# A gated mix of window attention and a gated MLP at decode: larger output-weight pieces, a one-row gate load, another order of two waits

## The chip, the cores and the metric

The kernel runs on one NeuronCore of a Trainium2 chip. The metric is the device time of one execution in microseconds (us). The kernel before takes 196.78 us, the median of four runs (196.64, 196.65, 196.91 and 196.96 us).

## The reference

One token per batch entry (B = 4, width 512) goes through two branches, and a scalar gate mixes them:

```python
g = sigmoid((x * gate_w).sum(-1))            # x: [4, 1, 512], gate_w: [512]
q = x @ wq                                   # 32 heads of 128; 8 key/value heads
k, v = the last 4096 rows of k_cache, v_cache
a = softmax(q k^T / sqrt(128)) v @ wo        # wq: [512, 4096], wo: [4096, 512]
b = (relu(x @ W_gate) * (x @ W_up)) @ W_down # 512 -> 1792 -> 512
out = g * a + (1 - g) * b                    # [4, 1, 512]
```

All tensors are bf16. The kernel reads 81 MB, nearly all of it the window of the two caches (8 blocks of 4 MB each for K and for V), wq and wo (4 MB each), and the three MLP matrices (1.8 MB each).

## The kernel before

The four engines and the SyncE queue (SP) each have a program written out in one fixed order (`_order` for the engines, `_dma_order` for SP), with semaphores between them. Every load is issued by SP on one queue. The order of the loads is: wq, x, gate_w, K0, K1, V0, then K and V blocks by turns up to K7 and V6, then W_gate and W_up, V7, W_down, and wo in pieces. A load of a block waits until its slot is free (four slots of 32 KB a partition in `slots`); the pieces of wo and W_down go to slots that came free long before.

Each block `s` holds four heads for one batch entry. VectorE (DVE) transposes K in four quarters (`EKT`, L492), TensorE (PE) makes the scores (`SC`), DVE adds a mask and takes the maximum (`ESC`, L528), ScalarE (ACT) takes the exponential (`EXP`, L620), DVE transposes the result (`EPT`, L543), and PE multiplies by V (`PV`, L394 by way of the helper at L321). One block's PV is issued while the next block's scores are made.

The start: `XT` (L334) transposes x with four small PE transposes into PSUM, `EXT` (L495) copies the result to `xT`, with four columns for each of the four quarters `q` of the width. ACT spreads gate_w over 128 columns (`GWB`, L600), and `Z` (L340) multiplies that by xT, which gives the logit of the gate on all partitions. Then `Q` (L345) makes the queries. PE runs these strictly in that order: CONST, XT, Z, Q. gate_w comes in as `gwT`, four elements (8 bytes) on each of 128 partitions.

The end: after block 7's scores PE runs `PV` of block 6, the fold of the row sums (`RS`), the two MLP products (`GU`), `PV` of block 7, `FFN` (the product with W_down, accumulated into a PSUM bank), `OQ` (brings the heads' outputs into the layout that wo needs), and `WO`: 64 matmuls with 256 columns each, numbered x = 0 to 63, that accumulate on FFN's result. `WO_PIECES` (L28) cuts these 64 into seven groups, and each group has a load of its own and waits for it alone (L427). A step of x is 512 bytes of every partition's row of wo, so the pieces are 8, 8, 8, 4, 2, 1.5 and 0.5 KB a partition. The last piece is loaded in three parts of 123, 3 and 2 partitions (`LOW3`). Last, ACT and DVE copy one half of the sum each to `osum` (`FIN`, L623 and L577), and SP issues the store (L285), which waits for both.

`E.wait` (L61) makes one wait for each semaphore, in the order in which the keys are given. In the program as it runs, the second of the store's two waits stands alone as an instruction ahead, and the first is carried by the store's own issue: the profile has a separate wait for DVE, and then the issue, which waits for ACT's semaphore.

Of the kernel before, what the change touches and what calls it, by code (L numbers as in the profile page):

```python
# [6 lines left out]
BF16 = mybir.dt.bfloat16  # L7
ACTF = mybir.ActivationFunctionType
# [16 lines left out]
OUTT = 2  # L25
OW = 512 // OUTT
OR = 128 // OUTT
WO_PIECES = ((0, 16), (16, 32), (32, 48), (48, 56), (56, 60), (60, 63), (63, 64))  # L28
LOW3 = (0, 123, 126, 128)

class _Plan:
# [18 lines left out]
def bc(ap, axis, n):  # L50
    shape = list(ap.shape)
    shape[axis] = n
    return ap.broadcast_to(shape)
# [49 lines left out]
def _alloc(nc, ctx):  # L103
    R = {}

    def sb(name, shape, dt):
        R[name] = ctx.enter_context(nc.sbuf_tensor(name, shape, dt))

    sb("slots", [128, NSLOT, 16384], BF16)
    sb("kt", [128, 4, 4096], BF16)  # L110
    sb("sc", [128, 2048], BF16)
    sb("pe", [128, 2048], BF16)
    sb("pT", [128, 2, 2048], BF16)
    sb("qblk", [128, NSET, 2, 144, 2], BF16)
    sb("xsb", [4, 512], BF16)
    sb("xT", [128, 16], BF16)
    sb("gwT", [128, 4], BF16)
    sb("osb", [128, NSET, 512], BF16)
    sb("oq", [128, 32, 4], BF16)
    sb("identb", [128, 128], BF16)  # L120
    sb("identf", [128, 128], FP32)
    sb("ones", [128, 128], FP32)
    sb("ee", [16, 128], BF16)
    sb("e4", [16, 128], BF16)
    sb("rfold", [128, 128], FP32)
    sb("grpb", [128, 128], BF16)
    sb("own8", [128, 8], FP32)
    sb("scl", [128, 8], FP32)
    sb("maskl", [128, 128], BF16)
    sb("maskr", [128, 512], BF16)  # L130
    sb("maskf", [128, 512], BF16)
    sb("gwB", [128, 4, 128], BF16)
    sb("fold", [128, 4, 4, 64], BF16)
    sb("mx4", [128, 4], FP32)
    sb("rd32", [128, 8, 4], BF16)
    sb("negmax", [128, 2], FP32)
    sb("rowsum", [128, NSET], FP32)
    sb("recip", [128, 4, 4], FP32)
    sb("ge", [128, 2, 4], FP32)
    sb("gp", [128, 2, 4], FP32)  # L140
    sb("gg", [128, 2, 4], FP32)
    sb("hg", [128, 14, 4], BF16)
    sb("osum", [4, 512], BF16)
    R["psum"] = ctx.enter_context(nc.psum_tensor("bank", [128, 8, 512], FP32))
    return R


def _order():
# [7 lines left out]
    o += [("SC", s, 3), ("SW", s), ("PV", s - 1), ("PT", s), ("RS", 1), ("GU",), ("PV", s), ("FFN",), ("OQ",)]  # L156
    return o + [("WO", p) for p in range(len(WO_PIECES))]


def _dma_order():  # L160
    o = [("wq",), ("x",), ("gw",), ("k", 0), ("k", 1), ("v", 0)]
    for s in range(2, NSET):
        o += [("k", s), ("v", s - 1)]
    return o + [("wg",), ("wu",), ("v", NSET - 1), ("wd",)] + [("wo", p) for p in range(len(WO_PIECES))]

# [22 lines left out]
def _program(nc, plan, R, aps):  # L188
    (A_x, A_k_cache, A_v_cache, A_wq, A_wo, B_W_gate, B_W_up, B_W_down, gate_w, out) = aps
    banks = [R["psum"][:, i, :] for i in range(8)]  # L190
    bankb = [b.bitcast(BF16) for b in banks]
    TR, SCB, ACC, OB = (0, 1), (2, 3, 4), 5, (6, 7)
    slots, kt, sc, pe, pT, qblk = R["slots"], R["kt"], R["sc"], R["pe"], R["pT"], R["qblk"]
    xsb, xT, gwT, osb, oq = R["xsb"], R["xT"], R["gwT"], R["osb"], R["oq"]
    identb, identf, ones = R["identb"], R["identf"], R["ones"]
    mx4, rd32, negmax, rowsum, recip = R["mx4"], R["rd32"], R["negmax"], R["rowsum"], R["recip"]
    ge, gp, gg, osum = R["ge"], R["gp"], R["gg"], R["osum"]
# [5 lines left out]
    def slot(*it):  # L203
        return slots[:, at[it], :]

    Wq = slot("wq").rearrange("p (t f) -> p t f", t=4)
# [22 lines left out]
    def tr(key):  # L229
        return TR[trf[key] % NTR]  # L230

    def tr_free(key):
        n = trf[key] - NTR
        return [("E",) + trk[n]] if n >= 0 else []

    def scb(key):
        return SCB[scf[key] % NSC]
# [5 lines left out]
    def wo_rows(p):  # L243

        return [slice(a, b) for a, b in zip(LOW3, LOW3[1:])] if p == len(WO_PIECES) - 1 else [slice(0, 128)]

# [6 lines left out]
    def sync(e):  # L253
        E = _Eng(plan, e, "sp")

        def load(ev, ctr, dst, src, waits=()):
            E.op(lambda: e.dma_start(dst, src), ev=ev, waits=waits, ctr=ctr)  # L257

        for it in _dma_order():
            k = it[0]  # L260
            w = slot_wait.get(it, [])
            if k == "x":
                load(("X",), "d_x", xsb[0:4, :], A_x.rearrange("b o d -> (b o) d"))
            elif k == "gw":
                load(("GW",), "d_gw", gwT[:, :], gate_w.rearrange("(p t) -> p t", t=4))
            elif k == "wq":
                load(("WQ",), "d_wq", slot("wq"), A_wq.rearrange("(p t) f -> p (t f)", t=4), waits=w)
            elif k == "wg":
                load(("WG",), "d_wg", Wg, B_W_gate.rearrange("(p t) f -> p (t f)", t=4), waits=w)
            elif k == "wu":  # L270
                load(("WU",), "d_wu", Wu, B_W_up.rearrange("(p t) f -> p (t f)", t=4), waits=w)
            elif k == "wd":
                load(("WD",), "d_wd", Wd, B_W_down.rearrange("(p i) c -> p (i c)", i=14),
                     waits=w)
            elif k == "wo":
                lo, hi = WO_PIECES[it[1]]
                wo = A_wo.rearrange("(p i) c -> p (i c)", i=32)
                for n, r in enumerate(wo_rows(it[1])):
                    load(("WO", it[1], n), f"d_wo{it[1]}", Wo[r, OW * lo:OW * hi], wo[r, OW * lo:OW * hi], waits=w)
            else:  # L280
                b, qq = set_of(it[1])
                src = (A_k_cache if k == "k" else A_v_cache)[b, 4 * qq:4 * qq + 4, SK - WIN:SK, :]
                load((k.upper(), it[1]), f"d_{k}{it[1] % 3}", slot(*it), src.rearrange("h (r c) d -> r h (c d)", r=32),
                     waits=w)
        load(("OUT",), "d_out", out.rearrange("b o d -> (b o) d"), osum[:, :], waits=[("OSUM", 0), ("OSUM", 1)])  # L285
        E.wait([("OUT",)])

    def gpsimd(e):
# [28 lines left out]
    def tensor(t):  # L317
        E = _Eng(plan, t, "pe")

        def mm(out_, lhsT, rhs, start, stop, ev=None, waits=(), pos=None):  # L320
            E.op(lambda: t.matmul(out_, lhsT, rhs, start=start, stop=stop, tile_position=pos, skip_group_check=True),  # L321
                 ev=ev, waits=waits)

        def tp(out_, in_, idn, ev=None, waits=()):
            E.op(lambda: t.transpose(out_, in_, idn), ev=ev, waits=waits)  # L325
# [8 lines left out]
        def XT():  # L334
            bk = bankb[tr(("XT",))]
            for q in range(4):
                tp(bk[:, 4 * q:4 * q + 4], xsb[0:4, q:q + 509:4], identb[0:4, 0:4], ev=("XT",) if q == 3 else None,
                   waits=tr_free(("XT",)) + [("X",), ("IDB",)])

        def Z():  # L340
            for q in range(4):
                mm(banks[ACC][:, 0:4], R["gwB"][:, q, :], xT[:, 4 * q:4 * q + 4], q == 0, q == 3, ev=("Z",) if q == 3 else None,
                   waits=[("E", "XT"), ("GWB",), ("INIT",)])

        def Q():  # L345
            for n in range(2):
                key = ("Q", n)
                for q in range(4):
                    for j in range(4):
                        c = (4 * n + j) * 512  # L350
                        mm(banks[scb(key)][32 * j:32 * j + 4, :], xT[:, 4 * q:4 * q + 4], Wq[:, q, c:c + 512],
                           q == 0, q == 3, ev=key if (q, j) == (3, 3) else None, pos=(0, 32 * j),
                           waits=sc_free(key) + [("WQ",), ("E", "XT"), ("INIT",)] if (q, j) == (0, 0) else ())

# [52 lines left out]
        def GU():  # L407
            for n, (W, key) in enumerate(((Wg, "WG"), (Wu, "WU"))):
                fill = ("GU", n)
                for q in range(4):  # L410
                    for j in range(4):
                        mm(banks[scb(fill)][32 * j:32 * j + 4, 0:448], xT[:, 4 * q:4 * q + 4],
                           W[:, FF * q + 448 * j:FF * q + 448 * j + 448], q == 0, q == 3,
                           ev=fill if (q, j) == (3, 3) else None, pos=(0, 32 * j),
                           waits=sc_free(fill) + [(key,)] if (q, j) == (0, 0) else ())
# [67 lines left out]
    def vector(v):  # L483
        E = _Eng(plan, v, "dve")
# [8 lines left out]
                 ev=("E", "KT", s, f), waits=w)  # L493

        def EXT():  # L495
            E.op(lambda: v.tensor_copy(xT[:, :], bankb[tr(("XT",))][:, 0:16]), ev=("E", "XT"), waits=[("XT",)])  # L496

        def EQ(n):
            key = ("Q", n)
# [86 lines left out]
    def scalar(a):  # L586
        E = _Eng(plan, a, "act")
# [10 lines left out]
            E.op(lambda: a.activation(dst[:, :], banks[tr(key)][:, 0:dst.shape[1]], ACTF.Copy), ev=("E",) + key, waits=[key])  # L598

        def GWB():  # L600
            E.op(lambda: a.activation(R["gwB"][:, :, :], bc(gwT[:, :].unsqueeze(2), 2, 128), ACTF.Copy), ev=("GWB",),  # L601
                 waits=[("GW",)])

        def NORM(s):
            E.op(lambda: a.activation(osb[:, s, :], ob(s), ACTF.Copy), ev=("NORM", s),  # L605
# [54 lines left out]
```

## Time and profile before

| what | value |
|---|---|
| profiled execution, its own time | 196.65 us |
| its span, first to last instruction | 195.4 us |
| time around the span | 1.25 us |
| PE busy | 121.4 us (62%) |
| DVE busy | 124.1 us (64%) |
| ACT busy | 27.5 us (14%) |
| DMA: data read, mean rate | 81.01 MB, 415 GB/s |
| DMA queue q1, share of 16 engines | 97.2% |
| mean granted PE clock | 0.904 |

The span is in us from the first instruction. A busy PE isn't a PE at its peak, as matmuls are pipelined and overlap. "Landing" is the moment at which a load's semaphore reaches its full count: each DMA engine that carried a part of it adds one when its part has been written, and the trace keeps each of these marks. A load over 128 partitions puts 8 partitions on each of 16 engines.

### The profile page before, as it was taken

The page shows a single profiled execution, that of the slowest core. Times are in us where ns is not written, and L with a number is a line of the kernel's source. Part 1 is how long each engine was busy: PE and PEld are TensorE (multiplying, and loading weights), DVE is VectorE, ACT ScalarE, POOL GpSimd, SP SyncE. Part 2 cuts the span into 40 slices and gives each one's busy share as a digit, 9 for nine tenths or more (in the row PEclk, how much of TensorE's full clock was granted, in tenths as well). Part 3 has the DMA queues.
Part 4 walks back from the last instruction along what each step waited for, and adds up shares of the span by engine and source line. Part 5 has one row for each costly group of instructions (what it writes and reads, how often), then busy time and mean ns, then how long its engine had stood idle before and what let it go on. Part 6 is the DMA issues. An engine that isn't in the chain of part 4 may idle for free.

```text
span 195.4 us, 1736 instructions
## 1 busy us (share of the span) xinstructions
PE 121.4 (62%) x723; PEld 51.1 (26%) x723; DVE 124.1 (64%) x153; ACT 27.5 (14%) x34; POOL 9.6 (5%) x25
## 2 busy tenths in 40 slices
PE   0218278465933894586367746894389456743976
PEld 0013123122411331142123311241134122311464
DVE  6104769999299819980998099819981998370010
ACT  2214000040130013001210131013001300420000
POOL 7830000000000000000000000000000000000000
PEclk9999958999999696999789987699969799996699
DMA  6999999999999999999999999999999999999992
GB/s 215 436 424 429 429 429 436 443 426 443 443 429 443 424 426 443 436 429 429 436 429 429 433 429 429 436 429 429 429 429 426 429 391 440 457 429 395 413 401 69
DMA packets 4046, 81.10 MB, mean 415 GB/s; under 512 B 576, under 2 KB 840, under 8 KB 1096
## 3 DMA queue, kind: packets, MB, share of 16 engines
q1 hardware_dynamic: 4040, 81.01, 97.2%
q8 instruction: 5, 0.08, 0.2%
q14 instruction: 1, 0.01, 0.0%
HBM read 81.01 MB, written 0.00 MB: 415 GB/s over the span
## 4 chain that ended last, share of the span: by engine, by line
DMA 65%; DVE 16%; PE 13%; issue 4%; SPq 0%; ACT 0%
DMA slots<-in_A_k_cache_dram 44%; DMA slots<-in_A_v_cache_dram 15%; DVE kt L492 13%; PE bank L321 13%; DMA gwT<-in_gate_w_dram 6%; DVE sc L528 2%; DVE oq L556 0%; SPq L257 0%; ACT gwB L601 0%; DVE rd L532 0%; DVE negmax L538 0%; DVE osum L578 0%; DVE mx L528 0%
## 5 line engine op out<-in xcount | busy, mean ns | idle before, releaser
L492 DVE STREAM_TRANSPOSE kt<-slots 128x2048 f32<-128x2048 f32 x32 | 73.7, 2306 | 28.6 <-DMA slots<-in_A_k_cache_dram 28.5
L321 PE MATMUL bank<-kt,qblk 128*128 128x512 bf16 x256 | 72.2, 433 | 28.1 <-DVE kt L492 28.1
L321 PEld LDWEIGHTS bank<-kt,qblk 128*128 128x128 bf16 x256 | 25.1, 107 | 70.0 <-DVE kt L492 36.4
L321 PE MATMUL bank<-slots,pT 128*64 128x512 bf16 x256 | 33.5, 421 | 5.7 <-DMA slots<-in_A_v_cache_dram 5.7
L620 ACT ACTIVATE pe<-sc,negmax 128x2048 bf16<-128x2048 bf16 x8 | 16.0, 2004 | 60.8 <-DVE negmax L538 60.8
L528 DVE CUSTOM_DVE_ANT_0 sc<-bank,maskf 128x512 bf16<-128x512 f32 x32 | 21.0, 658 | 3.9 <-PE bank L321 3.8
L321 PEld LDWEIGHTS bank<-slots,pT 128*64 128x64 bf16 x256 | 15.5, 121 | 24.0 <-issue 14.6
L543 DVE STREAM_TRANSPOSE pT<-pe 128x2048 bf16<-128x2048 bf16 x8 | 18.5, 2312 | 2.2 <-ACT pe L620 2.2
L605 ACT ACTIVATE osb<-bank 128x512 bf16<-128x512 f32 x8 | 4.8, 597 | 82.9 <-PE bank L321 82.9
L321 PE MATMUL bank<-rd,grpb 128*128 128x32 bf16 x8 | 1.6, 196 | 22.6 <-DVE rd L532 22.6
L556 DVE TENSOR_TENSOR oq<-bank,recip 64x128 bf16<-64x128 f32 x2 | 0.9, 434 | 13.6 <-PE bank L321 13.5
L321 PEld LDWEIGHTS bank<-rd,grpb 128*128 128x128 bf16 x8 | 0.8, 99 | 26.2 <-DVE rd L532 26.2
L496 DVE COPY xT<-bank 128x16 bf16<-128x16 bf16 x1 | 0.2, 167 | 8.3 <-PE bank L325 8.3
L321 PE MATMUL bank<-slots,xT 128*4 128x512 bf16 (+1 forms) x64 | 4.9, 462 | 0.0
L321 PE MATMUL bank<-slots,oq 128*4 128x256 bf16 x64 | 3.7, 272 | 1.1 <-DVE oq L556 1.1
L321 PE MATMUL bank<-maskr,maskl 128*128 128x512 bf16 x1 | 0.6, 608 | 5.9 <-POOL maskr L297 5.9
L518 DVE TENSOR_SCALAR qblk<-bank 32x64 uint32<-32x64 uint32 x16 | 2.9, 215 | 2.1 <-PE bank L325 2.1
L325 PE MATMUL bank<-identb,xsb 4*128 4x4 bf16 x4 | 0.3, 166 | 6.0 <-DMA xsb<-in_A_x_dram 6.0
L297 POOL TENSOR_SCALAR_AFFINE_SELECT fold<-fold 128x256 bf16<-128x256 bf16 x8 | 3.4, 419 | 1.1
L321 PEld LDWEIGHTS bank<-slots,oq 128*4 128x4 bf16 x64 | 2.8, 84 | 1.9 <-issue 1.3
L578 DVE CAST osum<-bank 4x256 bf16<-4x256 f32 x1 | 0.4, 419 | 3.9 <-PE bank L321 3.9
L487 DVE MEMSET qblk<- 128x2304 uint32 x1 | 2.0, 1978 | 1.3 <-PEq L645 1.3
(59 smaller groups left out, 40.4 us busy)
## 6 DMA issues: line engine op xcount, KB each, us to landing
slots<-in_A_k_cache_dram SPq DMA_DIRECT2D x8, 4096.0 KB, 25.4
slots<-in_A_v_cache_dram SPq DMA_DIRECT2D x8, 4096.0 KB, 31.0
slots<-in_A_wq_dram SPq DMA_DIRECT2D x1, 4096.0 KB, 12.5
slots<-in_A_wo_dram SPq DMA_DIRECT2D x3, 1024.0 KB, 16.4
slots<-in_B_W_gate_dram SPq DMA_DIRECT2D x1, 1792.0 KB, 19.7
slots<-in_B_W_up_dram SPq DMA_DIRECT2D x1, 1792.0 KB, 23.6
slots<-in_B_W_down_dram SPq DMA_DIRECT2D x1, 1792.0 KB, 18.5
slots<-in_A_wo_dram SPq DMA_DIRECT2D x1, 512.0 KB, 19.3
```

The lines of the kernel that those rows point to most:

```text
L297: op(lambda: e.affine_select(dst, src, pattern, cmp, fill, base=base, channel_multiplier=mult), ev)
L321: E.op(lambda: t.matmul(out_, lhsT, rhs, start=start, stop=stop, tile_position=pos, skip_group_check=True), ev=ev, waits=waits)
L325: E.op(lambda: t.transpose(out_, in_, idn), ev=ev, waits=waits)
L487: E.op(lambda: v.memset(qblk[:, :, :, :, :].rearrange("p s h c e -> p (s h c e)"), 0.0), ev=("QZ",))
L492: E.op(lambda: v.transpose(kt[:, f, :].bitcast(FP32), slot("k", s)[:, 4096 * f:4096 * f + 4096].bitcast(FP32)), ev=("E", "KT", s, f), waits=w)
L518: E.op(lambda dst=dst, r=r, g=g: v.tensor_scalar(dst, src[r, g, 0:B, :, :], 0, None, op0=ALU.bitwise_or), ev=("E",) + keys[1] if (q, g) == ...
L528: E.op(lambda: v.tensor_tensor_reduce(sc[:, 512 * f:512 * f + 512], banks[scb(key)], R["maskf"][:, :], 1.0, -3.0e38, ALU.add, ALU.max, mx4 ...
L543: E.op(lambda: v.transpose(pT[:, s % 2, :], pe[:, :]), ev=("E", "PT", s), waits=[("EXP", s)] + ([("PV", s - 2)] if s >= 2 else []))
L556: E.op(lambda g=g, r=r: v.tensor_tensor(oq[r, :, :].rearrange("p i b -> p b i"), banks[tr(key)][0:64, 128 * g:128 * g + 128].rearrange("p ...
L578: E.op(lambda: v.tensor_copy(osum[:, OW:2 * OW], banks[ACC][OR:OR + 4, 0:OW]), ev=("OSUM", 1), waits=[("WOP", len(WO_PIECES) - 1)])
L605: E.op(lambda: a.activation(osb[:, s, :], ob(s), ACTF.Copy), ev=("NORM", s), waits=[("PV", s)])
L620: E.op(lambda: a.activation(pe[:, :], sc[:, :], ACTF.Exp, bias=negmax[:, s % 2:s % 2 + 1], scale=SCALE, accum_out=rowsum[:, s:s + 1]), ev= ...
```

## The change

There are three parts.

1. `WO_PIECES` has five pieces in place of seven: x = 0 to 33, 34 to 51, 52 to 59, 60 to 62, and 63. In KB a partition: 17, 9, 4, 1.5 and 0.5. The last two are as before. All 64 matmuls stay, in the same order.
2. gate_w is loaded as one row of 1 KB into a fifth row of `xsb`, under the four rows of x. The four PE transposes take five rows, so that xT has five columns for each quarter, the fifth being gate_w. `GWB` reads these columns of xT, so it waits for `EXT` where it waited for the load of gate_w, and `XT` waits for gate_w's load in addition to x's. The PSUM columns are spaced by six, and `EXT` copies 20 of 24.
3. The store's waits are given in the order DVE, ACT (before: ACT, DVE).

```diff
-WO_PIECES = ((0, 16), (16, 32), (32, 48), (48, 56), (56, 60), (60, 63), (63, 64))
+WO_PIECES = ((0, 34), (34, 52), (52, 60), (60, 63), (63, 64))
...
-    sb("xsb", [4, 512], BF16)
-    sb("xT", [128, 16], BF16)
-    sb("gwT", [128, 4], BF16)
+    sb("xsb", [5, 512], BF16)
+    sb("xT", [128, 20], BF16)
...
-                load(("GW",), "d_gw", gwT[:, :], gate_w.rearrange("(p t) -> p t", t=4))
+                load(("GW",), "d_gw", xsb[4:5, :], gate_w.rearrange("(o p) -> o p", o=1))
...
-        load(("OUT",), "d_out", out.rearrange("b o d -> (b o) d"), osum[:, :], waits=[("OSUM", 0), ("OSUM", 1)])
+        load(("OUT",), "d_out", out.rearrange("b o d -> (b o) d"), osum[:, :], waits=[("OSUM", 1), ("OSUM", 0)])
...
-                tp(bk[:, 4 * q:4 * q + 4], xsb[0:4, q:q + 509:4], identb[0:4, 0:4], ev=("XT",) if q == 3 else None,
-                   waits=tr_free(("XT",)) + [("X",), ("IDB",)])
+                tp(bk[:, 6 * q:6 * q + 5], xsb[0:5, q:q + 509:4], identb[0:5, 0:5], ev=("XT",) if q == 3 else None,
+                   waits=tr_free(("XT",)) + [("X",), ("GW",), ("IDB",)])
...
-            E.op(lambda: v.tensor_copy(xT[:, :], bankb[tr(("XT",))][:, 0:16]), ev=("E", "XT"), waits=[("XT",)])
+            E.op(lambda: v.tensor_copy(xT[:, :].rearrange("p (q c) -> p q c", q=4), bankb[tr(("XT",))][:, 0:24].rearrange("p (q c) -> p q c", q=4)[:, :, 0:5]), ev=("E", "XT"), waits=[("XT",)])
...
-            E.op(lambda: a.activation(R["gwB"][:, :, :], bc(gwT[:, :].unsqueeze(2), 2, 128), ACTF.Copy), ev=("GWB",),
-                 waits=[("GW",)])
+            E.op(lambda: a.activation(R["gwB"][:, :, :], bc(xT[:, 4:20:5].unsqueeze(2), 2, 128), ACTF.Copy), ev=("GWB",),
+                 waits=[("E", "XT")])
```

In `Z`, `Q` and `GU` the matmuls read `xT[:, 5 * q:5 * q + 4]` in place of `xT[:, 4 * q:4 * q + 4]`.

More of the change, by code (lines that the diff above doesn't have):

```diff
@@ L193, in _program @@
     slots, kt, sc, pe, pT, qblk = R["slots"], R["kt"], R["sc"], R["pe"], R["pT"], R["qblk"]
-    xsb, xT, gwT, osb, oq = R["xsb"], R["xT"], R["gwT"], R["osb"], R["oq"]
+    xsb, xT, osb, oq = R["xsb"], R["xT"], R["osb"], R["oq"]
     identb, identf, ones = R["identb"], R["identf"], R["ones"]
@@ L336, in XT @@
             for q in range(4):
-                tp(bk[:, 4 * q:4 * q + 4], xsb[0:4, q:q + 509:4], identb[0:4, 0:4], ev=("XT",) if q == 3 else None,
-                   waits=tr_free(("XT",)) + [("X",), ("IDB",)])
+                tp(bk[:, 6 * q:6 * q + 5], xsb[0:5, q:q + 509:4], identb[0:5, 0:5], ev=("XT",) if q == 3 else None,
+                   waits=tr_free(("XT",)) + [("X",), ("GW",), ("IDB",)])
         def Z():
             for q in range(4):
-                mm(banks[ACC][:, 0:4], R["gwB"][:, q, :], xT[:, 4 * q:4 * q + 4], q == 0, q == 3, ev=("Z",) if q == 3 else None,
+                mm(banks[ACC][:, 0:4], R["gwB"][:, q, :], xT[:, 5 * q:5 * q + 4], q == 0, q == 3, ev=("Z",) if q == 3 else None,
                    waits=[("E", "XT"), ("GWB",), ("INIT",)])
@@ L350, in Q @@
                         c = (4 * n + j) * 512
-                        mm(banks[scb(key)][32 * j:32 * j + 4, :], xT[:, 4 * q:4 * q + 4], Wq[:, q, c:c + 512],
+                        mm(banks[scb(key)][32 * j:32 * j + 4, :], xT[:, 5 * q:5 * q + 4], Wq[:, q, c:c + 512],
                            q == 0, q == 3, ev=key if (q, j) == (3, 3) else None, pos=(0, 32 * j),
@@ L411, in GU @@
                     for j in range(4):
-                        mm(banks[scb(fill)][32 * j:32 * j + 4, 0:448], xT[:, 4 * q:4 * q + 4],
+                        mm(banks[scb(fill)][32 * j:32 * j + 4, 0:448], xT[:, 5 * q:5 * q + 4],
                            W[:, FF * q + 448 * j:FF * q + 448 * j + 448], q == 0, q == 3,
```

## The prediction

> **What bounds the kernel now.** I read the page's slices first, then the chain that ended last, then the timeline of both ends, then the issues with their landings, and last the windows of the tail. The slices of the page:
>
> ```profile
> PEclk9999958999999696999789987699969799996699
> DMA  6999999999999999999999999999999999999992
> GB/s 215 436 424 429 429 429 436 443 426 443 443 429 443 424 426 443 436 429 429 436 429 429 433 429 429 436 429 429 429 429 426 429 391 440 457 429 395 413 401 69
> ```
>
> The DMA engines are full from the first slice to the last but one (a slice is 4.9 us). From the first load to the landing of V7 the time is that of the stream of loads, and nothing else counts unless it empties the queue. The chain's last part, cut to the window from 178 us, shows what comes after V7:
>
> ```profile
> 149.57 29.33 DMA slots<-in_A_v_cache_dram
> 178.91 0.14 issue
> 179.04 9.80 PE bank L321 x76
> 188.84 0.02 issue
> 188.86 0.43 DVE oq L556
> 189.30 0.01 issue
> 189.31 0.45 DVE oq L556
> 189.76 0.14 issue
> 189.89 3.70 PE bank L321 x64
> 193.59 0.02 issue
> 193.62 0.42 DVE osum L578
> ```
>
> Columns are start, length, what. V7 lands at 178.91; then PV of block 7, FFN and OQ (9.80), two DVE copies (0.88), the 64 WO matmuls (3.70), the last copy, the store. Windows of the same stretch (length, then busy time and count of PE, PEld, DVE, ACT, POOL, granted clock, DMA share, GB/s):
>
> ```profile
> 177.60:181.00 3.40, 1.96 (x10) 1.04 (x12) 0.00 (x0) 0.00 (x0) 0.00 (x0) 0.50 0.96 407
> 181.00:184.40 3.40, 3.40 (x18) 1.65 (x16) 0.00 (x0) 0.00 (x0) 0.00 (x0) 0.50 1.02 420
> 184.40:189.80 5.40, 4.43 (x52) 3.07 (x48) 0.87 (x2) 0.60 (x1) 0.00 (x0) 0.99 0.99 410
> 189.80:193.60 3.80, 3.66 (x64) 2.76 (x64) 0.00 (x0) 0.02 (x1) 0.00 (x0) 1.00 0.44 160
> ```
>
> The reader is to see that PV of block 7 runs at half clock until 184.4, and that DMA is still moving wo while WO runs. So two things race to the end: PE, and the landing of wo's pieces. From the page's issues (KB, us from issue to landing):
>
> ```profile
> slots<-in_A_wo_dram SPq DMA_DIRECT2D x1, 256.0 KB, 19.4
> slots<-in_A_wo_dram SPq DMA_DIRECT2D x1, 192.0 KB, 19.4
> ```
>
> The 1.5 KB piece was issued at 173.69, so it landed at 193.09; the trace's matmul starts have x = 60, the first that needs it, at 193.165. The piece came first, by under 0.1 us. The 64 matmuls start in pairs 109 ns apart with no step at any border of a piece, so none waited and a group's waits cost PE nothing.
>
> **Part 1, the pieces of wo.** What a row costs an engine follows from landings, at 8 rows an engine and load. K and V: the chain has K4 landing at 92.59 and K6 at 131.45, four loads in 38.86 us, so 9.715 a load and 1.214 us for a 32 KB row. W_down lands at 183.20, 4.29 after V7: 0.536 us for 14,336 bytes. The second and third wo pieces land at 188.16 and 190.64: 0.310 us for 8,192 bytes. These lie on a line of 36.8 ns per 1000 bytes and 9 ns per row. Five large pieces become three, so each engine has 2 x 8 = 16 rows less: 16 x 9 ns = 0.15 us, and the last landing moves from 193.09 to 192.94. Bounds: 0 (rows above 8 KB no better) and 0.33 (all of wo, 258,048 bytes an engine in the 9.89 us between 183.20 and 193.09, at the rate of the 32 KB rows, 9.56). I take 0.15, since 17 and 9 KB lie between measured sizes. SP issues two loads less (about 0.43 us each), while it waits for nothing that is late.
>
> New waits: counted back from the last landing by the same line, the pieces would land at 188.4 (x = 0 to 33), 191.2 (34 to 51), 192.5 (52 to 59) and 192.94. PE at its present pace needs them at 189.9, 191.75, 192.73 and 193.165. The least slack is 0.2 us. Behind PE's wait for the first piece stands all of WO, and behind that FIN and the store; 1.5 us of slack cover it, and without them each us late would be a us of time. As PE isn't waiting now, the gain in this profile is 0; what it buys is cover for an earlier PE.
>
> **Part 2, gate_w as a row.** 128 packets of 8 bytes leave the stream between wq and K0, 8 on each engine. Their price: the 16 landing marks of wq run from 12.56 to 13.32, those of K0 from 22.41 to 23.11. Mark by mark in order, the difference has a median of 9.86, against 9.71 for the next loads: 0.15 for gate_w and x's four rows. x puts a row on four engines only, so I take 0.13 for gate_w. Bounds: 0.03 (the last marks differ by 9.79, so 0.08, less a 1 KB row at 9 + 38 = 47 ns if the last engine gets it) and 0.30 (the largest difference, 10.01). The queue never empties, so V7 lands 0.13 earlier, at 178.78, and all of wo too.
>
> On PE this is worth half: PV runs at half clock until a clock change at 184.45, which I take to stay where it is, so a start 0.13 earlier wins 0.065 of full-speed work. Bounds 0 and 0.13.
>
> The start gets longer. Before, GWB ran from 13.59 to 14.22 beside EXT (13.80 to 13.97); now it follows EXT: 13.97 + 0.05 + 0.63 = 14.65. Z moves from 14.36 to 14.79, and Q, queued behind Z on PE, ends at 18.2 in place of 17.76: 0.43 us late. XT's added wait for gate_w holds back XT, Z and Q: before, x landed near 13.4 and gate_w at 13.56, so at most 0.1 more. Then the queries, K0's transposes (23.13) and K2's issue (17.78) are 0.4 to 0.5 late. Cover: when K2 is issued, K0, K1 and V0 are still to come, to 43.47; when V1 is issued (34.90), K2 lies ahead until 53.19. DVE waits 3.53 us for K2 at 53.2, and there the delay is gone. Without that queue the whole 0.45 would be paid. Five columns in place of four in EXT (0.17 us) and the four transposes (0.17 us each), and weights that begin at multiples of 10 bytes, have no row; none to +0.1 us each, under the same cover. In GU the same weights run from 171.6 to 173.3, with PE idle until 179.04.
>
> **Part 3, the store.** The timeline's last lines (start, length):
>
> ```profile
> 193.58 0.37 ACT L624 ACTIVATE osum<-bank 4x256 bf16<-4x256 f32 x1 [7.61 <-PE bank L321]
> 193.62 0.42 DVE L578 CAST osum<-bank 4x256 bf16<-4x256 f32 x1 [3.87 <-PE bank L321]
> 194.13 0.27 SPq L257 DMA_DIRECT2D out_dram<-osum  x1
> ```
>
> DVE ends at 194.04, ACT at 193.95. The separate wait for DVE runs at 194.065, and the store's issue, with ACT's long satisfied wait, at 194.13. With the order turned, the separate wait is ACT's, done at about 193.97, and the issue waits for DVE itself. K2's issue, which carries its wait, starts 0.02 after PE's end (17.76 to 17.78). So 194.06 in place of 194.13: 0.065 won. Bounds 0 and 0.09. Behind it SP has only the wait for the store.
>
> **Sum.** In the profiled execution: 0.065 for V7, 0 for the pieces, 0.065 for the store: 196.65 - 0.13 = 196.52. That execution is one of the lower two of four; the others lie at 196.91 and 196.96, and the median 196.78 between. Where a run is bound by wo's landing instead, all counts: 0.13 + 0.15 + 0.065 = 0.35. Which of the two binds in which run one profile can't say, so I take 0.13 to 0.35 off the median, the middle: 196.55. About 0.2% (0.39 us) is what a measurement of this kernel can tell from no change, so this is no change.
>
> [...] The rows have the half clock from 177.6 to 184.4, 6.8 us. [...] The rows of x's load have four landing marks besides one bulk mark at issue. [...]
>
> **Rivals.**
> - *The landing binds, not PE* (0.31). For it: x = 60 began 0.08 us after its piece landed, and two of four runs lie within 0.01 us of each other, like a floor. Against it: no matmul waited. All runs would then go to 196.64 - 0.35 = 196.29: faster by 0.25%.
> - *The change does not do what it says* (0.12). The last engine sets every landing, and if gate_w's packets cost it only 0.03 and PE covers the pieces, only the store's 0.065 and some 0.02 are left: 196.70.
> - *A late engine* (0.08), slower. The packets of instructions (five of 16 KB in the page's queue q8) take 1.03 us each on one engine (the trace's packet times), and at the end one engine's V7 mark is 0.45 behind the next. With the program's length changed, one more on that engine moves wo's landing to 193.09 + 1.03 - 0.28 = 193.84, x = 60 to 0.7 after its present start, and the time to 196.65 + 0.70 - 0.07 = 197.28. It decides from 0.3 us of added lateness.
> - *The start shows* (0.05), slower. If the late Q and K0 reached the tail, +0.45 - 0.13 = +0.32, or more with the unknown small costs: 197.2. It would need the queue to run empty once; the shortest stretch between an issue and its landing among the K loads after K1, 23.5 us less its own 9.7, is far from that.
>
> **How the numbers follow.** No change by this sum has 0.44. Within 0.2%: 0.44 + 0.12 = 0.56; faster 0.31; slower 0.08 + 0.05 = 0.13. The likeliest is 196.55, with a range of its own from 196.35 to 196.75. The range reaches down to 196.15, for the second rival's floor with the larger bounds, and up to 196.95, which leaves out most of the slower cases.
>
> **What would show it.** Right: landing marks of K0 0.1 to 0.15 nearer to wq's; V7 landing near 178.8; Z near 14.8 and Q's end near 18.2 with V7 no later; WO's pairs at 109 ns with no step; the store 0.02 after DVE's end. Wrong: a step at x = 34 or 52, a wait of DVE for K2 that is longer than the load explains, one engine's marks a further us behind, or PV of block 7 at another clock, which would move the end by more than all the parts together.

## The result

The changed kernel takes 196.11 us (median of 38 runs, 195.94 to 196.74), against 196.68 us for the kernel before (58 runs, 196.31 to 197.78, taken with it). The ratio is 0.9972, with a 95% interval of 0.9967 to 0.9977: 0.28% or 0.55 us faster. The forecast was 196.55 us and no change, in a range from 196.15; the time lies 0.04 us below that range. All prices below are ratios times 196.68 us.

The profiled execution took 196.10 us with a span of 194.8 us, 0.55 us less than the one of before. DMA slices of the page, after:

```profile
DMA  6999999999999999999999999999999999998992
```

The engines are as full as before. The chain of what ended last, after, cut to the window from 176 us (start, length, what):

```profile
172.56 19.62 DMA slots<-in_A_wo_dram
192.18 0.04 issue
192.23 0.86 PE bank L320 x12
193.09 0.02 issue
193.11 0.42 DVE osum L577
```

Here is the first surprise. Before, the chain went from V7 over PE to the end; now it goes from the landing of a wo piece (x = 52 to 59, at 192.18) over twelve matmuls to the end. PE waits for wo. The timeline of the tail, after, shows where (start, length, engine, line, what, and in brackets the idle time before it and what ended it):

```profile
178.53 5.79 PE L320 MATMUL bank<-slots,pT 128*64 128x512 bf16 x32 [4.92 <-DMA slots<-in_A_v_cache_dram]
...
188.85 1.76 PEld L320 LDWEIGHTS bank<-slots,oq 128*4 128x4 bf16 x34 [1.30 <-DMA slots<-in_A_wo_dram]
188.88 3.13 PE L320 MATMUL bank<-slots,oq 128*4 128x256 bf16 x52 [1.06 <-DVE oq L555]
190.86 0.85 PEld L320 LDWEIGHTS bank<-slots,oq 128*4 128x4 bf16 x18 [0.26 <-DMA slots<-in_A_wo_dram]
192.22 0.53 PEld L320 LDWEIGHTS bank<-slots,oq 128*4 128x4 bf16 x12 [0.51 <-DMA slots<-in_A_wo_dram]
192.23 0.82 PE L320 MATMUL bank<-slots,oq 128*4 128x256 bf16 x12 [0.22 <-DMA slots<-in_A_wo_dram]
193.08 0.37 ACT L623 ACTIVATE osum<-bank 4x256 bf16<-4x256 f32 x1 [8.12 <-PE bank L320]
193.11 0.42 DVE L577 CAST osum<-bank 4x256 bf16<-4x256 f32 x1 [4.38 <-PE bank L320]
193.56 0.27 SPq L256 DMA_DIRECT2D out_dram<-osum  x1
```

WO begins at 188.88, a whole us earlier than before (189.89), stops before x = 34 and before x = 52, and ends half a us earlier. It began so early because V7 landed at 178.40 in place of 178.91, and because the half-clock stretch ended earlier. Windows, after (columns as before: length, busy time and count of PE, PEld, DVE, ACT, POOL, granted clock, DMA share, GB/s):

```profile
176.10:179.51 3.41, 0.98 (x6) 0.57 (x8) 0.00 (x0) 0.00 (x0) 0.00 (x0) 0.50 0.98 418
179.51:182.93 3.42, 3.42 (x20) 1.65 (x18) 0.00 (x0) 0.00 (x0) 0.00 (x0) 0.50 1.03 435
182.93:188.80 5.87, 4.88 (x58) 3.37 (x54) 0.87 (x2) 0.60 (x1) 0.00 (x0) 1.00 0.97 407
188.80:193.10 4.30, 3.95 (x64) 2.53 (x64) 0.00 (x0) 0.02 (x1) 0.00 (x0) 1.00 0.52 201
```

Full clock is back at 182.93, not at 184.45. By the trace's marks the pieces of 4 KB and 1.5 KB a partition landed at 192.18 and 192.62, the latter 0.47 us earlier than before.

So the stream of loads reached its end 0.47 us earlier, 0.06 more came from the store, and the stream's lead was there when V7 landed (0.51). The question for the runs is which edit moved the stream, since the forecast had 0.13 for the gate load up to V7.

### The profile page after: what moved, and what is told of

It reads as the page before. It is cut to its first block, busy times and chain, and to the rows that moved or that the text cites. A ratio compares the mean times of both kernels' runs of the same rounds, so it can differ in the third digit from the quotient of the medians.

```text
span 194.8 us, 1734 instructions
## 1 busy us (share of the span) xinstructions
PE 124.1 (64%) x723; PEld 51.3 (26%) x723; DVE 124.4 (64%) x153; ACT 27.5 (14%) x34; POOL 9.6 (5%) x25
## 4 chain that ended last, share of the span: by engine, by line
DMA 54%; DVE 31%; PE 9%; issue 4%; SPq 0%; ACT 0%
DMA slots<-in_A_k_cache_dram 38%; DVE kt L491 21%; DMA slots<-in_A_wo_dram 10%; PE bank L320 8%; DMA xsb<-in_A_x_dram 6%; DVE sc L527 5%; PE bank L324 1%; DVE qblk L517 1%; DVE pT L542 1%; DVE rd L531 1%; SPq L256 0%; DVE negmax L537 0%; ACT gwB L600 0%; DVE osum L577 0%; DVE mx L527 0%
## 5 line engine op out<-in xcount | busy, mean ns | idle before, releaser
L320 PE MATMUL bank<-kt,qblk 128*128 128x512 bf16 x256 | 73.5, 438 | 30.8 <-DVE kt L491 30.8
```

## The experiments

Theories at the start: A, each part is worth what the forecast's rows give; B, the gate load is worth nearly all; C, it is chance, by where instruction packets fall. Each trace is one execution; "last mark" is the landing on the last of the 16 engines, "mean mark" the mean over the 16. A price that is the difference of two runs has the errors of both.

**The five pieces alone.**

```diff
-WO_PIECES = ((0, 16), (16, 32), (32, 48), (48, 56), (56, 60), (60, 63), (63, 64))
+WO_PIECES = ((0, 34), (34, 52), (52, 60), (60, 63), (63, 64))
```

> The five pieces of wo alone, with gate_w on 128 partitions and the store's waits as before. Theory A (each part is worth what it takes off the last engine's stream): 16 rows less at 9 ns, so wo's last landing 0.15 us nearer to V7's, and 0 to 0.15 us off the time. Rival B (the 8-byte packets of gate_w are nearly all of the gain): 0 to 0.05 us off. Rival C (the gain of 0.57 us is where instruction packets fall on the DMA engines, by the program's length): anything from 0 to 0.5 us off, with V7's last landing mark moved and K0's not.

Measured: ratio 1.0004 (0.9995 to 1.0013), so +0.08 us (-0.10 to +0.26). No gain shows. From V7's first mark to that of x = 60 to 62, on the engine that is first each time, 14.26 us became 14.08, about what 16 rows less at 9 ns give (0.15). From V7's last mark to the piece's last mark it was 14.18 and is 14.12 here, 14.22 in the changed kernel. Over all thirteen traces of this document it has a median of 14.21 in the five with seven pieces and 14.11 in the eight with five, so that some 0.1 us remains on the last engine too. In the trace of this run, WO waits for its pieces before x = 34 and x = 52 although gate_w comes in the old form: V7 landed late (179.17), and full clock was back at 182.88.

**The gate row alone.** All of the change but the pieces and the order of the store's waits.

```diff
-                load(("GW",), "d_gw", gwT[:, :], gate_w.rearrange("(p t) -> p t", t=4))
+                load(("GW",), "d_gw", xsb[4:5, :], gate_w.rearrange("(o p) -> o p", o=1))
...
```

> gate_w as one row under x alone, with seven pieces and the store's waits as before. Theory A: K0 and V7 land 0.13 us earlier, 0.13 to 0.25 us off the time; Q ends at 18.2 in place of 17.76 and nothing is paid for that. Rival B: V7 and wo land 0.4 to 0.5 us earlier, 0.4 to 0.5 us off the time. Rival C: as the change has it by chance, from 0 to 0.5 us off, with marks of K0 that are 0.13 us earlier and marks of V7 that differ more.

Measured: 0.9982 (0.9973 to 0.9991), so -0.35 us (-0.53 to -0.18). V7's last mark is 178.44 (before 178.91), the last wo mark 192.64 (193.09). Those landings, 0.47 and 0.45 earlier, are rival B's; the time lies between A's and B's, and its interval reaches into both. The timeline of its tail shows PE's weight loads waiting for wo three times:

```profile
191.59 0.31 PEld L320 LDWEIGHTS bank<-slots,oq 128*4 128x4 bf16 x8 [0.50 <-DMA slots<-in_A_wo_dram]
...
192.24 0.09 PEld L320 LDWEIGHTS bank<-slots,oq 128*4 128x4 bf16 x4 [0.34 <-DMA slots<-in_A_wo_dram]
192.68 0.09 PEld L320 LDWEIGHTS bank<-slots,oq 128*4 128x4 bf16 x4 [0.35 <-DMA slots<-in_A_wo_dram]
```

So with seven pieces too it is the landing that ends the run.

**The store's order alone.**

```diff
-        load(("OUT",), "d_out", out.rearrange("b o d -> (b o) d"), osum[:, :], waits=[("OSUM", 0), ("OSUM", 1)])
+        load(("OUT",), "d_out", out.rearrange("b o d -> (b o) d"), osum[:, :], waits=[("OSUM", 1), ("OSUM", 0)])
```

> The order of the store's two waits alone. All theories: the store's issue starts 0.02 us after VectorE's last copy ends in place of 0.09, so 0.065 us off the time. The stream of loads is that of the kernel before, so the trace also shows how much the landing marks of wq, K0, V7 and wo differ between two executions with the same loads: theory A says under 0.1 us for the last marks, rival C says up to 0.5 us.

Measured: 0.9989 (0.9980 to 0.9999), so -0.22 us (-0.39 to -0.02). By the trace the issue starts 0.027 us after DVE's end, where it was 0.092: 0.065, inside that interval. Its loads are those of before, and its marks agree with them to 0.1: K0 23.01 (23.11), V7 178.86 (178.91), wo 193.10 (193.09). Yet here a weight load waited for the landing, before x = 60, where none did in the profile of before:

```profile
193.15 0.09 PEld L321 LDWEIGHTS bank<-slots,oq 128*4 128x4 bf16 x4 [0.21 <-DMA slots<-in_A_wo_dram]
```

Full clock was back at 184.30, 0.15 us earlier than in that profile. The kernel with the pieces alone has the same loads up to V7, but K0 at 23.90 and V7 at 179.17. So the last marks differ by up to 0.9 us at K0 between executions that load gate_w in the old form, and this is there before the first 16 KB instruction packet (39 us).

**The old gate load twice**, in the kernel before.

```diff
                 load(("GW",), "d_gw", gwT[:, :], gate_w.rearrange("(p t) -> p t", t=4))
+                load(("GW2",), "d_gw2", R["gwT2"][:, :], gate_w.rearrange("(p t) -> p t", t=4))
```

> The kernel before with the load of gate_w to 128 partitions issued twice, the second copy unread: the disputed cost doubled. Theory A: K0 and V7 land 0.13 us later, and the time is 0.07 to 0.13 us longer. Rival B: V7 lands 0.4 us or more later, and the time is 0.3 to 0.5 us longer. Rival C: no shift of the time beyond 0.1 us.

Measured: 1.0046 (1.0033 to 1.0059), so +0.90 us (0.65 to 1.16), more than any theory said. K0's last mark is 24.35, V7's 180.00. Theories A and C fall. The place is visible in the windows of the stream, 12 to 16 us, in which the gate load passes, and 16 to 24. Before:

```profile
12.00:16.00 4.00, 1.90 (x24) 0.92 (x28) 0.17 (x1) 0.87 (x3) 0.08 (x1) 1.00 0.95 395
16.00:24.00 8.00, 3.92 (x36) 2.13 (x28) 5.26 (x21) 1.88 (x1) 0.00 (x0) 1.00 1.06 459
```

After:

```profile
12.00:16.00 4.00, 1.86 (x24) 0.92 (x28) 0.17 (x1) 0.87 (x3) 0.09 (x1) 1.00 1.03 444
16.00:24.00 8.00, 4.74 (x40) 2.59 (x28) 4.55 (x21) 1.88 (x1) 0.00 (x0) 1.00 1.01 434
```

With the old load twice:

```profile
12.00:16.00 4.00, 2.00 (x24) 0.91 (x28) 0.17 (x1) 0.87 (x3) 0.05 (x1) 1.00 0.85 337
16.00:24.00 8.00, 4.10 (x36) 2.13 (x28) 4.39 (x20) 1.88 (x1) 0.00 (x0) 1.00 1.02 438
```

The last two columns are what counts. With two loads the engines are idle for part of the first window, and the packets' own 9 ns each don't show it: over both windows 0.40 MB fewer moved than after, 0.9 us of the stream. With one load the first window alone misleads: before has 49 GB/s less than after in it, but 25 more in the second, and over the 12 us both moved 5.25 MB. Sixteen packets of 32 KB are 0.5 MB, so which of them fall into a window of 4 us moves its figure by as much as the load is worth. The landing marks of K0, shown in a table below, carry the price of a single load.

For the next runs the theory was D: the landing ends the run, the gate row is worth 0.35 to 0.5 us, the pieces little.

**The changed kernel with seven pieces.** The first diff above, backwards.

> The changed kernel with the old seven pieces of wo, so gate_w's row and the store's order remain. Theory D (the landing of wo on its last engine ends every run; the gate row is worth 0.35 to 0.5 us, the store 0.06, the pieces at most 0.1): within 0.1 us of the changed kernel, so 0.4 to 0.55 us under the kernel before. Rival E (the pieces are worth 0.15 to 0.2 once the gate row has moved V7): 0.3 to 0.4 us under the kernel before.

Measured: 0.9978 (0.9968 to 0.9987), so -0.43 us (-0.63 to -0.26) against before, 0.12 us more than the changed kernel, with intervals that overlap. D's figure against before fits, and 0.12 is its 0.1 within the error; E, 0.15 to 0.2 for the pieces, isn't excluded. V7's last mark is 178.63, that of wo 192.87.

**The old gate load added, unread.** In the changed kernel, behind the gate row.

```diff
+                load(("GW2",), "d_gw2", R["gwT2"][:, :], gate_w.rearrange("(p t) -> p t", t=4))
```

> The changed kernel with one more load behind gate_w's row: gate_w on 128 partitions of 8 bytes, as the kernel before had it, unread. Theory D (the 8-byte packets hold their engines for far more than the time of the packets): K0's last mark 0.3 to 1.0 us later than in the changed kernel, and 0.35 to 0.6 us more time, so about 0.1 us under to 0.1 us over the kernel before. Theory A, as predicted: 0.13 us more. Rival G (what cost the time was the wait of the gate chain on that load, not its packets): no more time.

Measured: 1.0001 (0.9991 to 1.0012), 0.57 us more than the changed kernel. All of the gain is gone, though nothing waits for this load, and K0's last mark is 0.48 us later than in the changed kernel (23.18 against 22.70). Rival G falls, and A's 0.13 too.

**128 rows of 512 bytes added, unread**, in the same place.

```diff
+                load(("GW2",), "d_gw2", R["gwT2"][:, :], B_W_gate[0:128, 0:256])
```

> The changed kernel with one more unread load behind gate_w's row: 128 rows of 512 bytes of W_gate, 64 KB, as many rows as gate_w had on 128 partitions and 64 times the bytes. By the line of 9 ns a row and 36.8 ns per 1000 bytes: 8 x 28 ns = 0.22 us more. Theory D: 0.2 to 0.3 us, less than the 8-byte load costs. Rival F (any load of 128 short rows costs the same there, whatever their size): as much as the 8-byte load, 0.35 to 0.6 us.

Measured: 0.9988 (0.9979 to 0.9997), 0.31 us more than the changed kernel, where the line of rows and bytes has 0.22. The intervals of this and the last run overlap a little, so both were made fourfold below.

**Three more matmuls on PE in the last stretch** of the changed kernel.

```diff
+                if x == 0:
+                    for _ in range(3):
+                        mm(banks[tr(("OQ",))][0:4, 256:512], oq[:, 0, :], Wo[:, 0:OW], True, True, pos=(0, 0))
```

> The changed kernel with three more matmuls of 256 columns, into an unused part of a bank, behind the first matmul of WO: 0.33 us more work on TensorE in the race at the end. Theory D (the landing ends the run; PE waits 0.2 us before x = 34 and 0.5 us before x = 52 in the changed kernel): 0 to 0.1 us more. Rival: PE's chain sets the end, 0.33 us more.

Measured: 0.9975 (0.9964 to 0.9986), 0.06 us more than the changed kernel, against 0.33 if PE's chain set the end. So in the changed kernel PE's chain doesn't set the end. Its timeline still has PE's weight loads wait for wo, with the same 0.51 us before x = 52:

```profile
192.37 0.53 PEld L320 LDWEIGHTS bank<-slots,oq 128*4 128x4 bf16 x12 [0.51 <-DMA slots<-in_A_wo_dram]
```

**Four loads of three shapes**, unread, behind the gate row of the changed kernel: 128 partitions of 8 bytes, 128 of 512 bytes, 16 of 64 bytes. Three kernels, each with one of these lines four times.

```diff
+                load(("GW2", 0), "d_gw2", R["gwT2"][:, 0, :], gate_w.rearrange("(p t) -> p t", t=4))
...
+                load(("GW2", 0), "d_gw2", R["gwT2"][:, 0, :], B_W_gate[0:128, 0:256])
...
+                load(("GW2", 0), "d_gw2", R["gwT2"][:, 0, :], gate_w.rearrange("(p t) -> p t", t=32))
...
```

> The changed kernel with four unread loads of gate_w on 128 partitions of 8 bytes behind the gate row (one such load cost 0.57 us more than the changed kernel). Theory A, 9 ns a row and engine: 4 x 8 x 9 = 0.3 us more than the changed kernel. Theory D, a price of 0.35 to 0.6 us for each load of 128 packets: 1.4 to 2.4 us more, seen in K0's landing marks.

Measured: 1.0087 (1.0068 to 1.0106), 2.26 us more than the changed kernel, 0.57 a load.

> The changed kernel with four unread loads of 128 rows of 512 bytes behind the gate row (one cost 0.31 us). By the line of rows and bytes, 4 x 0.22 = 0.9 us more than the changed kernel. Theory D: 0.9 to 1.2 us, less than four loads of 8-byte packets. Rival F (any 128 short rows cost the same): as much as the four 8-byte loads, 1.4 to 2.4 us.

Measured: 1.0029 (1.0016 to 1.0042), 1.12 us more, 0.28 a load. Rival F falls.

> The changed kernel with four unread loads of gate_w on 16 partitions of 64 bytes behind the gate row: one packet an engine and load in place of eight. Theory D (the price goes with the packets): an eighth of the price of the 8-byte loads, 0.2 to 0.3 us more than the changed kernel. Rival H (the price is that of a load, its issue and its semaphore): as much as four 8-byte loads, 1.4 to 2.4 us.

Measured: 0.9986 (0.9977 to 0.9996), 0.28 us more, 0.07 a load. Rival H falls: the price goes with the packets, not with the load. The windows with the four 8-byte loads:

```profile
12.00:16.00 4.00, 1.68 (x24) 0.78 (x27) 0.17 (x1) 0.87 (x3) 0.05 (x1) 1.00 0.67 256
16.00:24.00 8.00, 5.13 (x40) 2.93 (x32) 4.19 (x20) 1.88 (x1) 0.00 (x0) 0.94 1.01 438
```

The 8-byte loads bring the stream down to 256 GB/s and two thirds of its share for 4 us, and the next window doesn't make up for it: 0.72 MB fewer than after, 1.7 us. The marks, in us, where several values stand in the order of the kernels named:

| loads | K0, mean mark | K0, last mark | V7, last mark |
|---|---|---|---|
| one gate row (changed kernel, row alone, seven pieces, PE extra) | 22.46, 22.47, 22.48, 22.48 | 22.70, 22.80, 22.84, 22.81 | 178.40, 178.44, 178.63, 178.66 |
| 128 x 8 bytes once (before, store alone, pieces alone, added to the row) | 22.71, 22.58, 23.05, 22.80 | 23.11, 23.01, 23.90, 23.18 | 178.91, 178.86, 179.17, 178.96 |
| 128 x 8 bytes twice | 23.56 | 24.35 | 180.00 |
| row, and 128 x 8 bytes four times (the shortest of its runs, 197.79 us) | 24.28 | 25.46 | 179.98 |
| row, and 128 x 512 bytes once, four times | 22.69, 23.40 | 23.06, 24.08 | 178.80, 179.89 |
| row, and 16 x 64 bytes four times | 22.64 | 22.95 | 178.51 |

With the row alone the mean mark of K0 agrees to 0.02 us between four executions. One load of 8-byte rows moves it by 0.10 to 0.57 us, 0.31 on average: the price differs from execution to execution. The four 8-byte loads move it by 1.81 us (0.45 a load), the four 512-byte loads by 0.93 (0.23 a load, the 0.22 of rows and bytes), the four 64-byte loads by 0.17 (0.04 a load). Per packet on an engine (eight in a load of 128 rows, one in a load of 16) that is 57, 29 and 42 ns by these marks, and 71, 35 and 70 ns by the times. The last figure is loose: with the errors of both runs, 0.28 us for four loads may be 0.07 to 0.49.

## Why the prediction missed

- **The step that failed: "so I take 0.13 for gate_w".** In its place the runs showed 0.35 us for taking the load away (0.18 to 0.53) and 0.57 for adding it, alone or by fours. The sign and the mechanism, tiny packets in a full stream, were right; the term was taken at 0.23 to 0.37 of its size. The working compared K0's marks with wq's, mark by mark, in one execution, and its own sign came true: the median difference went from 9.86 to 9.72, 0.14 nearer. But three things spoil it as a price. First, one execution isn't the price: one such load moved K0's mean mark by 0.10 to 0.57 us in four traces, and before, with 0.23, is one of the cheaper. Second, the end waits for the last engine, not the median: K0's last mark is 0.41 us earlier after than before, V7's 0.51; over the table's first two rows the averages differ by 0.52 and 0.44. Third, wq's own marks are not a clean start: wq's mean mark is 12.83 before and 12.73 after, and its last mark is 13.32 and 13.30 in two of the four traces with the old load in line behind x, and 13.01 to 13.12 in the four with the row alone. Why wq is late there wasn't tried. With 0.35 to 0.57 in place of 0.13, the forecast's own sum for a run that wo's landing binds would have been 0.57 to 0.79 with its 0.15 for the pieces, and 0.42 to 0.64 without; 0.55 was measured.
- **"On PE this is worth half."** It took the clock change to stay at 184.45. It came at 182.93 after, and between 182.3 and 185.1 over all traces. With an early change PE waits for wo, and then the landing's lead counts in full. The first rival said so, with 0.31; the 0.08 us by which x = 60 came after its piece in the one profile of before was a near tie, not PE's rule. The store's order alone, with the same loads and matmuls, shows it: there PE's weight load waited for that piece. In ten of the thirteen traces a weight load of WO waited for a piece. The three others (before and the two with a single unread load) had full clock back at 184.45 to 184.8, so both cases occur.
- **The pieces.** 0.15 on an engine was about right (14.26 to 14.08 us on the first one, some 0.1 on the last over all traces). In time it bought nothing alone and 0.12 us in the changed kernel against the seven pieces, both within the error, so between "the gain in this profile is 0" and the 0.15 the runs don't decide. The steps at x = 34 and 52, which the forecast named as a sign of failure, came, because PE arrived a us earlier; the pieces landed 0.3 to 0.4 us before the forecast's times. (By the forecast's own line the third piece lands at 192.4, not 192.5; nothing hangs on it.)
- **The start.** The mechanism was right, the moment came out partly by luck. GWB follows EXT, so Z starts 1.27 us after XT (13.13 to 14.40), before 0.85 (13.51 to 14.36): 0.42 longer, as forecast. First the line of Q before, then GWB, Z, Q and K2's issue after:

```profile
14.54 3.19 PE L321 MATMUL bank<-slots,xT 128*4 128x512 bf16 x32
```

```profile
13.63 0.63 ACT L600 ACTIVATE gwB<-xT 128x512 bf16<-128x512 bf16 x1 [5.79 <-DVE xT L495]
14.40 0.25 PE L320 MATMUL bank<-xT,gwB 128*128 128x4 bf16 x4 [1.02 <-ACT gwB L600]
14.58 3.58 PE L320 MATMUL bank<-slots,xT 128*4 128x512 bf16 x32
...
18.21 0.53 SPq L256 DMA_DIRECT2D slots<-in_A_k_cache_dram  x1
```

  Z starts at 14.40 rather than 14.79, as x landed 0.3 us earlier, and Q took 3.58 us rather than 3.19 (full clock is first on record at 19.09 us in this trace, at 17.20 before). The two cancel, so that K2's issue came at 18.21, as forecast; with the pieces alone, where gate_w comes in the old form, Q took 3.58 us too and K2's issue came at 18.34. K0's transposes were 0.7 us late (23.84 against 23.13), more than the forecast's 0.5. V7 was none the later for any of it. The row of gate_w went through one engine: its load has one landing mark (12.99) besides a bulk mark at its issue.
- **The store.** Right to the digit: 0.065 us.
- **The slower rivals** (a late engine, the start) didn't occur. The sum as the runs have it: 0.35 to 0.57 for the gate load, 0.065 for the store and 0 to 0.12 for the pieces, 0.42 to 0.76 together, against 0.55 in all.

## What to carry to other kernels

A load of many tiny rows inside a full stream is not to be priced by the packets' own durations (9 ns each here, 0.07 us for the eight on an engine), nor by one execution, nor by the GB/s of a few us, whose figure hangs on which large packets fall into it. Compare the landing marks of the next large load, mean and last, over several executions with and without it. Here 128 rows of 8 bytes (1 KB) cost 0.35 to 0.57 us, the time of 150 to 245 KB at 430 GB/s. In this kernel it paid to bring such a vector in as one row and to turn it with a transpose that runs anyway. Where two chains end within 0.1 us of each other in one profile, neither may be called the bound: forecast for both, as the next execution can fall the other way.

## What the runs showed of the hardware

With four such loads an 8-byte packet cost its engine 57 ns by K0's mean marks (13 to 71 in the traces with one load) and 71 ns by the times, a 512-byte packet 29 and 35, a 64-byte packet some 42 (loose by the times), though the trace gives 9, 27 and 11 ns for these packets themselves. So 512-byte packets cost about what the line of rows and bytes gives (28 ns), and 8-byte packets several times what it gives (9 ns); the 64-byte figure points the same way (42 ns by the marks, where the line gives 11). Why is not shown, and no run has a size between 64 and 512 bytes. The loads of 8 and of 64 bytes all read the same 1 KB, those of 512 bytes didn't, and no run separates this from the size.

The moment at which full clock came back in the tail lay anywhere from 182.3 to 185.1 us in traces with almost the same work. Three whose PV of block 7 began within 0.12 us of each other (178.53 in the changed kernel, 178.58 with the row alone, 178.65 with the four 64-byte loads) had it at 182.93, 182.31 and 183.78. So in these traces the start of the work didn't fix the moment; what did is not shown.
